# One written order for five engines: prelude, batch 0 and the start of batch 1 of a fused attention and expert kernel

## The chip, the cores and the metric

The kernel runs on one core of one Trainium2 chip. The metric is device time in microseconds (us) of one execution. Five engines run their own instruction lists and wait for each other on semaphores: TensorE (PE in the rows, its weight loads PEld), VectorE (DVE), ScalarE (ACT), GpSimd (POOL) and SyncE (SP), which here issues all transfers.

## What is computed

Three layers follow each other. The first is Nystrom attention over 8 batches, 8 heads, 576 tokens and 64 dimensions, with 32 landmarks (means of 18 tokens) and six steps of a Newton iteration for an inverse:

```python
A, Bm, C = sm(q, k_lm), sm(q_lm, k_lm), sm(q_lm, k)     # softmaxes
Z = Bm.T / (norm_1(Bm) * norm_inf(Bm) + 1e-6)
for _ in range(6):
    Z = 2 * Z - Z @ Bm @ Z
attn = A @ Z @ C @ v
x = silu(attn @ w_gate) * (attn @ w_val) @ w_out        # 512 -> 1536 -> 512
```

The third is a soft mixture of 8 experts with 4 slots each: logits `x @ phi`, a softmax over tokens that gathers 32 slot inputs, two products per expert, and a softmax over slots that spreads the results over the 4608 tokens.

## The kernel before, in words

The output of the attention is never formed. Per batch the kernel makes `WB = Z C v` in small (its last product is `m_w`, its copy L538), multiplies it with a chunk of gate and value weights (`g_product`, L758: `g`), splits `g` in a high part `GH` (ScalarE, L775) and a low part `GL` (VectorE, L789), and multiplies both with the high and low part of the softmax `A` (`EH`, `EL`) in `mm3` (L955). A batch has 12 units, one for each 128 of the 1536 hidden columns. A unit has two halves of 288 tokens; a half is a product `pg` (gate), `u = silu(pg)` on ScalarE (L313), a product `pv` (value) and `hT = u * pv` on VectorE (L984). `hT` goes into the logits (L804) and is transposed into `HB` (L809). There are two buffers each of `pg`, `pv`, `u` and `hT`.

The **prelude** (`first_attention`) does batch 0's attention with nothing of the units beside it: landmark sums of q and k (L334), score products `m_a` and `m_c` (L544) and the 32x32 landmark scores (L378), their softmax (`nrm`, L310, L448 to L451), block-diagonal tiles `bd` (L323), the norms `nx` and the factor `rc` (L477, L328), the first Newton tile (L482), five squarings `m_n` whose halves are copied by VectorE (L505) and ScalarE (L506), products `m_T`, then `VD` (L529) and `m_w`. The softmax of A runs beside it, with subtractions, multiplications and the low part `EL` on GpSimd (L730, L733, L736).

In the prelude and batch 0 the weights are prepared too. They lie in memory as 64-bit numbers. Gate and value weights come in 12 chunks of 1 MB (`HB` or `wr`, L204), the output weights in 12 of 512 KB (L215). A conversion has a ScalarE pass (L177), for some chunks another one (L184), and VectorE passes (L193 with L194, or L190). The output weights are then transposed (`m_wt`), multiplied with phi (`m_p`, `m_ps`) and stored back. The 12 chunks of both kinds must be ready unit by unit in batch 0, where the attention of batch 1 runs as well.

What sets the order: the code is traced in one sequence, with the side work placed by the numbers in `SCHED`. A scheduler then orders each engine's instructions, held by `keep_order` for TensorE from the first unit on (L1154) and for ScalarE within batch 0 (L1115), and by single constraints `issue_after`. The order is fixed when the program is built; on the chip each engine takes its list in order.

Of the kernel before, what the change touches and what calls it, by code (L numbers as in the profile page):

```python
# [51 lines left out]
}  # L52


@with_exitstack
def nystrom_softmoe_kernel(
    ctx: ExitStack,
# [13 lines left out]
    nc = tc.nc  # L71
    pe, act, dve, pool, sp = nc.tensor, nc.scalar, nc.vector, nc.gpsimd, nc.sync

    def keep_order(engine, start, end):

        last = None
        for i in nc.cur_bb.bb.instructions[start:end]:
            if i.engine == engine:
                if last is not None:
                    tc.add_manual_dep(i, last.name, mybir.DependencyInfo(  # L80
                        mybir.DependencyClass.NoSync, mybir.DependencyReason.DATA), reason="keep_order")
                last = i

    def open_pool(name, bufs=1, **kw):
        return ctx.enter_context(tc.tile_pool(name=name, bufs=bufs, **kw))
# [71 lines left out]
    def load_four(nm, b):  # L157

        for hp in range(4):
            t = ap.tile([128, S], F32, tag="qk", name=f"{nm}{b}_{hp}", bufs=4)  # L160
            sp.dma_start(t, (qT if nm == "q" else kT)[b, hp])
            qk_t[nm, b, hp] = t

    def load_v(b):
        t = ap.tile([128, 5, DM], F32, tag="v", name=f"v{b}", bufs=1)
        sp.dma_start(t[:, 0:4, :], v[b, 0:512].rearrange("(c p) d -> p c d", p=128))
        sp.dma_start(t[0:64, 4, :], v[b, 512:576])
        v_t[b] = t
# [32 lines left out]
    def load_w(j):  # L201
        g = W_STAGE[j]
        t = (big(g, f"wr{j}") if g[0] == "w" else part(int(g[0]), int(g[1]))).bitcast(U64)
        sp.dma_start(t, w_cat[j])  # L204
        raw["w", j] = t
# [86 lines left out]
    for j in range(NJ):  # L292
        for kind in "wo":
            first, span = S_[kind][j]
# [8 lines left out]


    fence = {}

    def in_order(kind, *a, **kw):
        other = fence.get("exp" if kind == "silu" else "silu")
        if other is None:
            i = act.activation(*a, **kw)  # L310
        else:
            with tc.issue_after(other):
                i = act.activation(*a, **kw)  # L313
        fence[kind] = getattr(i, "ins", i)

# [14 lines left out]

    def landmark(nm, b, hp, dst):

        with tc.issue_after(fence["hT" if b == 2 else "sum"]) if "sum" in fence else nullcontext():
            dve.tensor_reduce(dst[:, hp, :], qk_t[nm, b, hp].rearrange("p (m s) -> p m s", s=SEG),  # L334
                              axis=AX.X, op=ALU.add)

# [9 lines left out]
    def e_tiles(b):  # L346
        r = []
        for low in range(2):
            p, tag = e_space(b, low)
            r.append(p.tile([128, 2 * S], F32R, tag=tag, name=tag).rearrange("p (q s) -> p q s", q=2))  # L350
        E_t[b] = r
# [356 lines left out]
    def a_softmax(b, qs=(0, 1)):  # L708
        AN, mxA = A_t[b]

        assert b == 0 or ("A", b, 1) in seq
        bc = {q: mxA[:, q, :].unsqueeze(2).to_broadcast([128, SEG, M]) for q in qs}
        at = {}

        def inv(q):
            mx = mxA[:, q, :]
            with tc.issue_after(fence["stat" if b > 1 else "hT"]) if b else nullcontext():
                dve.tensor_reduce(mx, AN[q], axis=AX.X, op=ALU.add)
            dve.tensor_scalar(mx, mx, 1e-9, None, ALU.add)
            dve.reciprocal(mx, mx)  # L720

        def back(q):
            at[q] = ap.tile([128, S], F32, tag="AT", name="AT", bufs=2)
            if b not in E_t:
                e_tiles(b)
            with tc.issue_after(fence["hT"]) if b == 1 else nullcontext():
                dve.transpose(at[q].rearrange("p (t r) -> p t r", r=32), AN[q])

        for f in (lambda q: dve.tensor_reduce(mxA[:, q, :], AN[q], axis=AX.X, op=ALU.max),
                  lambda q: pool.tensor_tensor(out=AN[q], in0=AN[q], in1=bc[q], op=ALU.subtract),  # L730
                  lambda q: in_order("exp", AN[q], AN[q], AF.Exp, scale=SC / SEG),
                  inv,
                  lambda q: pool.tensor_tensor(out=AN[q], in0=AN[q], in1=bc[q], op=ALU.mult),  # L733
                  back,
                  lambda q: act.copy(E_t[b][0][:, q, :], at[q]),
                  lambda q: pool.tensor_tensor(out=E_t[b][1][:, q, :], in0=at[q], in1=E_t[b][0][:, q, :],  # L736
                                               op=ALU.subtract)):
            for q in qs:
                f(q)
                yield  # L740
        if 1 in qs:
            seq.add(("asm", b))
# [35 lines left out]
    def g_unit(b, j):  # L778

        if not paired(b, j):  # L780
            g_product(b, j, 1)
        elif j % 2 == 0:
            g_product(b, j, 2)
# [3 lines left out]
    def g_low():  # L787
        for GL, g, GH in gl_todo:
            dve.tensor_tensor(out=GL, in0=g, in1=GH, op=ALU.subtract)  # L789
        gl_todo.clear()  # L790
# [4 lines left out]
    def logits(b, j, hT):  # L795
        if j == 0:
            L_t[b] = psp.tile([128, 512], F32, tag="l", name="l")
        assert j in p_done
        L = L_t[b]
        seq.add(("l", b, j))  # L800
        main = hT.rearrange("p (k c r) -> p k c r", k=5, c=4)
        for c in range(4):
            k = 5 if c < 2 else 4
            pe.matmul(L[32 * c:32 * c + 32, 0:32 * k], P_sb[:, j, :], main[:, 0:k, c, :],  # L804
                      start=j == 0, stop=j == NJ - 1)

    def transposes(b, j, hT):
        seq.add(("h", b, j))
        dve.transpose(HB[b % 2][:, S * j:S * j + S].rearrange("p (t r) -> p t r", r=32),  # L809
                      hT[:, 0:S].rearrange("p (t r) -> p t r", r=32))  # L810
# [192 lines left out]
    for x in S_["loads"]:  # L1003
        k, n = x[0], x[1:]
# [21 lines left out]
                next(gens[c], None)  # L1026

    m = psp.tile([128, 512], F32, tag="l", name="warm")
    for _ in range(14):
        pe.matmul(m[0:1, 0:1], one, one, start=True, stop=True)  # L1030
    first_attention(side)
    in_order("silu", warm, one, AF.Silu)
# [27 lines left out]
    last = nb - 1  # L1060
# [20 lines left out]
    def tail_loads(b, n):  # L1081
        if b == last - 1 and n == 47:
            attn_stack.close()
            fwp.append(open_pool("fw", side="right", reuse_waits="tile"))
            for t in range(NW):
                ffn_prefetch(t)
        if b == last:
            if n == 26:
                for t in range(NW, NW + 3):
                    ffn_prefetch(t)  # L1090
            if n % 8 == 6:
                i = n // 8
                if i < 3:
                    wo_load(i)
                elif i < 6:
                    ffn_prefetch(NW + i)
# [12 lines left out]
            todo[48 * a + r].append(sm)  # L1109
    prev = None  # L1110
    n_ins = lambda: len(nc.cur_bb.bb.instructions)
    middle = n_ins()
    for b in range(nb):
        if b == 1:
            keep_order(mybir.EngineType.Activation, middle, n_ins())  # L1115
        for j in range(NJ):
            p = prev
            def slot(i):
                n = 4 * j + i
                sg, sl, st_, first = S_["u0" if b == 0 else "u"]  # L1120
                if first:
                    for gen in todo[48 * b + n]:
                        next(gen, None)
                if i == sg and j + 1 < NJ:
                    g_unit(b, j + 1)
                if i == sl and p:
                    logits(*p)
                if i == sg + 1:
                    g_low()
                if i == st_ and p:  # L1130
                    transposes(*p)
                if b == 0:
                    for f in side_w[n]:
                        f()
                if (b, n) == (0, 1):
                    load_w(5)
                if b == 0 and nb > 2:
                    if n == S_["lq"]:
                        assert ("q", 1) in seq
                        load_four("k", 2)  # L1140
                    if n == S_["lv"]:
                        assert ("v", 1) in seq
                        load_v(2)
                tail_loads(b, n)
                if not first:
                    for gen in todo[48 * b + n]:
                        next(gen, None)
                if n == 45 and b + 1 < nb:
                    g_unit(b + 1, 0)
                if n == 46:  # L1150
                    g_low()

            prev = (b, j, *unit(b, j, slot))
    keep_order(mybir.EngineType.PE, middle, n_ins())  # L1154
    in_order("exp", warm, one, AF.Exp)
    logits(*prev)
    transposes(*prev)
# [205 lines left out]
```

## Time and profile before

| | us |
|---|---|
| median of 3 runs (lowest, highest) | 658.64 (657.75, 659.1) |
| the profiled execution, its own time | 659.78 |
| its span, first to last instruction | 658.0 |
| TensorE busy, VectorE busy, ScalarE busy, GpSimd busy in it | 622.5, 468.6, 302.2, 72.3 |

The profiled execution is 1.14 us above the median; 1.78 us of it lie outside the span. A busy engine in this table is one for which the profile shows an instruction under way, and a matmul's shown end is modelled, so short waits of TensorE can lie inside its busy time.

### The profile page before, as it was taken

What the parts mean: (1) busy time and instruction counts of PE and PEld (TensorE: products, weight loads), DVE (VectorE), ACT (ScalarE), POOL (GpSimd) and SP (SyncE); (2) the same over time, 40 slices, a digit from 0 to 9 for tenths busy, and PEclk for the clock granted to TensorE, in tenths of its full rate; (3) what the DMA queues carried; (4) which work ended last, traced back from release to release, by engine and by line L of the source; (5) the groups of instructions that cost most, each with busy time, mean ns of one, the idle gap of its engine ahead of it and who ended that gap; (6) DMA issues with size and microseconds to landing.
All of it is one profiled execution on the core that took longest, in us unless ns stands there. A gap on an engine that the chain in (4) does not pass through costs nothing. (4 is left out here: it accounts for less than half of the span.)

```text
span 658.0 us, 18310 instructions
## 1 busy us (share of the span) xinstructions
PE 622.5 (95%) x7587; PEld 471.1 (72%) x7587; DVE 468.6 (71%) x1139; ACT 302.2 (46%) x761; POOL 72.3 (11%) x81
## 2 busy tenths in 40 slices
PE   7899999999999999999999999999999999999990
PEld 4765678777777787778787778777878877743660
DVE  5898989987678597859785978697866656550441
ACT  2657976365338233823482347234723442311540
POOL 0401012003013001300130013001300000010100
PEclk9799989999999999999999999999999999999996
DMA  8998872542031223112321241122220696599998
GB/s 308 387 327 278 291 248 86 160 148 86 1 99 63 74 75 122 51 63 73 115 73 48 74 143 24 68 73 74 58 89 2 196 376 225 189 333 347 348 371 306
DMA packets 63299, 106.48 MB, mean 162 GB/s; under 512 B 4976, under 2 KB 33008, under 8 KB 61680
## 3 DMA queue, kind: packets, MB, share of 16 engines
q1 hardware_dynamic: 63216, 105.32, 47.7%
q8 instruction: 59, 0.97, 0.6%
q14 instruction: 24, 0.20, 0.1%
HBM read 91.24 MB, written 12.58 MB: 158 GB/s over the span
## 5 line engine op out<-in xcount | busy, mean ns | idle before, releaser
L313 ACT ACTIVATE u<-pg 128x288 f32<-128x288 f32 x169 | 69.7, 412 | 156.4 <-PE pg L955 152.7
L984 DVE TENSOR_TENSOR hT<-u,pv 128x288 f32<-128x288 f32 x169 | 75.8, 448 | 42.3 <-PE pv L955 36.7
L955 PE MATMUL pg<-EH,GH 128*128 128x288 f32 x384 | 94.2, 326 | 0.5 <-ACT GH L775 0.5
L789 DVE TENSOR_TENSOR GL<-g,GH 128x512 fp32r<-128x512 f32 (+1 forms) x114 | 64.7, 597 | 37.0 <-ACT GH L775 36.9
L955 PE MATMUL pg<-EH,GL 128*128 128x288 f32 x384 | 85.3, 299 | 1.7 <-DVE GL L789 1.2
L955 PE MATMUL pv<-EL,GH 128*128 128x288 f32 x384 | 82.4, 296 | 0.0
L955 PE MATMUL pv<-EH,GH 128*128 128x288 f32 x384 | 82.4, 296 | 0.0
L955 PE MATMUL pg<-EL,GH 128*128 128x288 f32 x384 | 82.3, 296 | 0.0
L955 PE MATMUL pv<-EH,GL 128*128 128x288 f32 x384 | 82.1, 295 | 0.0
L775 ACT CAST GH<-g 128x512 fp32r<-128x512 f32 (+1 forms) x114 | 53.4, 520 | 55.3 <-PE g L758 55.2
L955 PEld LDWEIGHTS pg<-EH,GH 128*128 128x128 f32 x384 | 59.6, 190 | 24.7 <-issue 20.3
L809 DVE STREAM_TRANSPOSE HB<-hT 128x576 f32<-128x576 f32 x96 | 74.3, 774 | 1.8
L955 PEld LDWEIGHTS pg<-EH,GL 128*128 128x128 f32 x384 | 62.4, 188 | 4.3 <-DVE GL L789 4.2
L955 PEld LDWEIGHTS pv<-EH,GH 128*128 128x128 f32 x384 | 61.8, 189 | 0.0
L955 PEld LDWEIGHTS pv<-EH,GL 128*128 128x128 f32 x384 | 61.8, 189 | 0.0
L955 PEld LDWEIGHTS pg<-EL,GH 128*128 128x128 f32 x384 | 61.8, 189 | 0.0
L955 PEld LDWEIGHTS pv<-EL,GH 128*128 128x128 f32 x384 | 61.7, 189 | 0.0
L758 PE MATMUL g<-w,WB 64*32 64x512 f32 (+1 forms) x912 | 56.7, 534 | 0.5 <-DVE w L190 0.5
L804 PEld LDWEIGHTS l<-hT,P_sb 128*32 128x32 f32 x768 | 15.2, 108 | 43.8 <-DVE hT L984 14.9
L804 PE MATMUL l<-hT,P_sb 128*32 128x160 f32 (+1 forms) x768 | 44.8, 298 | 1.4 <-DVE hT L984 1.1
L923 PE MATMUL m_d<-HB,HB 32*32 32x384 f32 x864 | 35.3, 491 | 0.0
L923 PE MATMUL m_d<-HB,DN 32*32 32x384 f32 x288 | 35.1, 491 | 0.0
(254 smaller groups left out, 955.8 us busy)
## 6 DMA issues: line engine op xcount, KB each, us to landing
k<-in_kT_dram SPq DMA_DIRECT2D x52, 288.0 KB, 3.7
ffn<-in_w_dram SPq DMA_DIRECT2D x13, 1024.0 KB, 8.3
ffn<-in_w_dram SPq DMA_DIRECT2D x24, 512.0 KB, 9.0
HB<-in_w_cat_dram SPq DMA_DIRECT2D x8, 1024.0 KB, 7.7
v<-in_v_dram SPq DMA_DIRECT2D x8, 1024.0 KB, 6.0
q<-in_qT_dram SPq DMA_DIRECT2D x28, 288.0 KB, 3.0
HB<-in_w_out_dram SPq DMA_DIRECT2D x12, 512.0 KB, 5.3
wr<-in_w_cat_dram SPq DMA_DIRECT2D x4, 1024.0 KB, 8.8
```

Source lines behind the costliest of these rows:

```text
L313: i = act.activation(*a, **kw)
L758: pe.matmul(gs[r][32 * hp:32 * hp + 32, 0:256 * n].rearrange("p (u f) -> p u f", u=n), WB[b % 2][64 * r:64 * r + 64, hp, :], w[64 * r:64 * ...
L775: act.copy(H_, g)
L789: dve.tensor_tensor(out=GL, in0=g, in1=GH, op=ALU.subtract)
L804: pe.matmul(L[32 * c:32 * c + 32, 0:32 * k], P_sb[:, j, :], main[:, 0:k, c, :], start=j == 0, stop=j == NJ - 1)
L809: dve.transpose(HB[b % 2][:, S * j:S * j + S].rearrange("p (t r) -> p t r", r=32), hT[:, 0:S].rearrange("p (t r) -> p t r", r=32))
L923: pe.matmul(ms[a][32 * g:32 * g + 32, 0:384].rearrange("p (j f) -> p j f", j=NJ), d_of(a, g, k), hb[32 * a:32 * a + 32, :, 4 * k + g, :], ...
L955: pe.matmul(ps[:, 0:HALF], G_t[b, j, q, sel_][h], e[:, q, ts_], start=n == 0, stop=n == 5)
L984: i = dve.tensor_tensor(out=o, in0=u, in1=pv[:, 0:HALF], op=ALU.mult)
```

## The change

`ORDER` holds a list of numbers for each engine. A number is an instruction's place among those traced for that engine, and `a+n` is a run of n from place a. `written_order` chains the listed instructions in that order. The lists have 928 entries for TensorE, 263 for VectorE, 182 for ScalarE, 18 for GpSimd and 72 for SyncE, and cover the prelude, batch 0 and the first units of batch 1. What is not listed comes behind the last listed one, on TensorE in traced order, on the others as the scheduler puts it. The two calls of `keep_order` go. The `issue_after` constraints of activation functions, landmarks and A's softmax are dropped for what is traced before unit 1 of batch 1. Two one-column warm-up products are added (14 to 16). No other instruction is added or removed, and no tile changes its buffer.

```diff
+ORDER = {
+    'DVE': '''
+      1 0 4 3 2 6 5 7 24 12 61 9 8 10 23 14+2 11 17 22 16 18+3 27 21 13 42+2 25+2 32+7 41 29 39 44+2 49 46
...
+    def written_order():
+        for name, runs in ORDER.items():
+            traced = [i for i in nc.cur_bb.bb.instructions if i.engine == getattr(mybir.EngineType, name)
+                      and type(i).__name__.startswith("Inst")]
+            first, last = [], None
+            for r in runs.split():
+                a, n = (int(x) for x in (r + "+1").split("+")[:2])
+                first += traced[a:a + n]
+            for i, before in zip(first[1:], first):
+                behind(i, before)
+            seen = {i.name for i in first}
+            last = first[-1]
+            for i in traced:
+                if i.name not in seen:
+                    behind(i, last)
+                    if name == "PE":
+                        last = i
...
-    for _ in range(14):
+    for _ in range(16):
         pe.matmul(m[0:1, 0:1], one, one, start=True, stop=True)
...
-    middle = n_ins()
     for b in range(nb):
-        if b == 1:
-            keep_order(mybir.EngineType.Activation, middle, n_ins())
         for j in range(NJ):
+            if (b, j) == (1, 1):
+                written[0] = False
...
-    keep_order(mybir.EngineType.PE, middle, n_ins())
+    written_order()
```

Lines of the changed kernel stand about 60 higher than those of before (L505 becomes L567, L194 becomes L252, L184 becomes L242).

**VectorE, from the norms to the first Newton tile, and the five squarings.** Before, from the maximum over C's scores on (`CE`; `mxA` and `AN` belong to A's softmax):

```order
L395 TENSOR_REDUCE stat<-CE_159 128x1
L477 TENSOR_REDUCE nx<-m_nx 128x4
L396 TENSOR_SCALAR stat<-stat 128x1
L718 TENSOR_REDUCE mxA<-AN_156 128x18
L328 TENSOR_SCALAR rc<-nx 128x1 x2
L719 TENSOR_SCALAR mxA<-mxA 128x18
L395 TENSOR_REDUCE stat<-CE_160 128x1
L329 RECIPROCAL rc<-rc 128x2
L720 RECIPROCAL mxA<-mxA 128x18
L482 SCALAR_TENSOR_TENSOR newton<-m_n,rc,cst 128x128 x2
```

In the change, the same stretch:

```order
L791 TENSOR_REDUCE mxA<-AN_158 128x18
L457 TENSOR_REDUCE stat<-CE_162 128x1
L458 TENSOR_SCALAR stat<-stat 128x1
L457 TENSOR_REDUCE stat<-CE_161 128x1
L458 TENSOR_SCALAR stat<-stat 128x1
L539 TENSOR_REDUCE nx<-m_nx 128x4
L390 TENSOR_SCALAR rc<-nx 128x1 x2
L391 RECIPROCAL rc<-rc 128x2
L544 SCALAR_TENSOR_TENSOR newton<-m_n,rc,cst 128x128 x2
```

Nothing stands between the norms and the Newton tile any more. The second reduction of `mxA`, for which GpSimd's subtractions wait, has moved from ahead of the scaling of `nrm` to behind it.

**VectorE, from the last squaring's copy to the first unit's low parts, in the change** (L567 is the copy, L251 and L252 are conversion passes of weight chunk `w_251`, L396 landmark sums of batch 1):

```order
L567 COPY newton<-m_n 128x128
L251 TENSOR_SCALAR w_251<-w_251 128x512 x2
L252 SCALAR_TENSOR_TENSOR w_251<-HB_84,w_251 128x512
L396 TENSOR_REDUCE qs<-q_1_113 128x32
L396 TENSOR_REDUCE ks<-k_0_111 128x32
L591 TENSOR_SCALAR VD<-m_v_445,rc 128x64 x2
L252 SCALAR_TENSOR_TENSOR w_251<-HB_84,w_251 128x512
L396 TENSOR_REDUCE ks<-qk_123 128x32
L252 SCALAR_TENSOR_TENSOR w_251<-HB_84,w_251 128x512
L851 TENSOR_TENSOR GL<-g,GH 128x256 x2
```

Before, `VD` follows the last copy directly and the conversion of that chunk is done ahead of both; now five 512-column passes of it and two landmark sums stand between and behind.

**ScalarE, around the first squaring's copy.** Before:

```order
L177 ACTIVATE HB_85<-HB_85 128x512
L310 ACTIVATE CE_160,stat<-CE_160,stat 128x576
L506 COPY newton<-m_n 128x128
L313 ACT_TABLE_LOAD
L313 ACTIVATE warm<-one 1x1
L177 ACTIVATE w_249<-HB_84 128x1024
L495 COPY newton<-m_T 128x256
```

In the change (`wr_131` is the raw chunk 4 of the gate and value weights, not touched here before):

```order
L372 ACTIVATE CE_161,stat<-CE_161,stat 128x576
L372 ACTIVATE AN_159<-AN_159 128x576
L242 ACTIVATE wr_131<-wr_131 128x1024
L568 COPY newton<-m_n 128x128
L472 COPY CT<-m_t 128x512
L235 ACTIVATE w_668<-wr_131 128x1024
L568 COPY newton<-m_n 128x128
```

The load of the activation table for silu has gone from here to just ahead of the first unit's `u`, and a pass over chunk 4 stands ahead of the copy.

## Rows read from the trace of the kernel before

**Rows 1.** Windows of four stages: us; PE, PEld, DVE, ACT, POOL; clock, DMA share, GB/s.

```profile
0.00:39.49 39.49, 31.43 (x325) 22.77 (x325) 29.58 (x69) 17.94 (x43) 9.02 (x14) 0.91 0.96 348
39.49:122.58 83.09, 78.67 (x869) 60.96 (x869) 74.68 (x167) 60.96 (x137) 8.76 (x7) 0.98 0.68 233
122.58:190.88 68.30, 66.50 (x859) 51.70 (x858) 53.44 (x132) 31.02 (x81) 10.58 (x10) 1.00 0.30 92
190.88:256.04 65.16, 64.98 (x827) 51.08 (x825) 51.19 (x127) 29.35 (x77) 8.27 (x8) 1.00 0.25 78
```

**Rows 2.** Timeline of TensorE: the first product of batch 0 and of batch 1.

```profile
39.49 0.68 PE L955 MATMUL pg<-EH,GH 128*128 128x288 f32 x2 [0.52 <-ACT GH L775]
...
122.58 0.52 PE L955 MATMUL pg<-EH,GH 128*128 128x288 f32 x2
```

**Rows 3.** Waits of VectorE up to 123 us: us in total, times, longest.

```profile
DVE qs L334 <- DMA q<-in_qT_dram: 3.9, 2, 3.6
DVE GL L789 <- ACT GH L775: 3.3, 3, 1.4
DVE AN L390 <- PE m_a L544: 2.3, 1, 2.3
DVE newton L505 <- PE m_n L471: 2.1, 2, 1.1
DVE u L970 <- ACT u L969: 1.2, 1, 1.2
DVE hT L984 <- ACT u L313: 1.1, 2, 0.7
...
DVE VD L529 <- PE m_v L526: 0.6, 1, 0.6
...
DVE AN L390 <- ACT nrm L310: 0.4, 1, 0.4
```

**Rows 4.** Timeline of VectorE in the prelude: start, us, instructions.

```profile
14.59 0.12 DVE L448 TENSOR_SCALAR stat<-stat 128x2 f32<-128x2 f32 x1
...
16.37 1.82 DVE L451 TENSOR_SCALAR nrm<-nrm,stat 128x32 f32<-128x32 f32 x2
...
18.64 0.38 DVE L455 TENSOR_SCALAR nrm<-cst,stat 128x32 f32<-128x32 f32 x2
...
31.33 1.16 DVE L194 SCALAR_TENSOR_TENSOR w<-HB,w 128x512 int32<-128x512 int32 x1
32.41 1.37 DVE L519 TENSOR_SCALAR stat<-stat 128x2 f32<-128x2 f32 x1
...
35.60 0.48 DVE L529 TENSOR_SCALAR VD<-m_v,rc 128x64 f32<-128x64 f32 x2 [0.56 <-PE m_v L526]
```

**Rows 5.** Timeline of GpSimd in the prelude: the subtractions and the low parts.

```profile
15.88 2.27 POOL L730 TENSOR_TENSOR AN<-AN,mxA 128x576 f32<-128x576 f32 x2 [14.71 <-DVE stat L449]
...
30.52 3.23 POOL L736 TENSOR_TENSOR EL<-AT,EH 128x576 fp32r<-128x576 f32 x2 [4.82 <-ACT EH L735]
```

**Rows 6.** Groups of ScalarE's instructions up to 122.58 us: busy us, mean ns.

```profile
L313 ACT ACT_TABLE_LOAD x3 | 3.8, 1283 | 0.1
...
L184 ACT ACTIVATE wr<-wr 128x1024 int32<-128x1024 uint16 x2 | 2.3, 1164 | 0.0
```

**Rows 7.** Windows, columns as in rows 1: the first 20 us, and a stretch at the lower clock.

```profile
0.00:10.00 10.00, 6.39 (x71) 2.88 (x74) 5.53 (x8) 1.49 (x2) 0.58 (x7) 1.00 0.84 295
10.00:20.00 10.00, 8.99 (x84) 6.59 (x74) 7.28 (x23) 4.45 (x11) 2.27 (x2) 1.00 0.95 349
22.60:29.40 6.80, 5.91 (x27) 5.31 (x27) 4.73 (x13) 5.14 (x11) 2.42 (x3) 0.50 1.04 381
```

**Rows 8.** Transfers issued up to 125 us: KB each, median us to landing.

```profile
HB<-in_w_cat_dram SPq DMA_DIRECT2D x8, 1024.0 KB, 7.7
HB<-in_w_out_dram SPq DMA_DIRECT2D x12, 512.0 KB, 5.3
wr<-in_w_cat_dram SPq DMA_DIRECT2D x4, 1024.0 KB, 8.8
...
q<-in_qT_dram SPq DMA_DIRECT2D x8, 288.0 KB, 3.3
...
cst<-in_consts_dram SPq DMA_DIRECT2D x1, 209.0 KB, 5.7
```

More of the change, by code (lines that the diff above doesn't have):

```diff
@@ L52 @@
 }
+ORDER = {
+    'PE': '''
[7 rows of a table added]
+      788+4 820+6 832+8 814+6 826+6 844+12 862+6 872+16 856+6 888+8 840+4 896+6 920+8''',
+    'DVE': '''
[8 rows of a table added]
+      239 242+2 238 241 240 247+2 255 252 256+2 253 259 249 246 258 262 261''',
+    'Activation': '''
[5 rows of a table added]
+      162 167 166 168+2 171 173 170 174 172 175 181 177 176 180 179''',
+    'Pool': '''
+      0 2+6 1 8 10 9 11 16 12 15 13+2 17''',
+    'SP': '''
+      0+2 5 2+2 7 4 6 14 26 8 15 18 10 25 22 17 16 20 9 23 11+3 40 24 19 21 29+2 28 32+2 31 34 36 35 37+3
+      42 41 58 43 45 44 27 46 59+2 47+2 61 50+2 49 64 52 65 53 56+2 66+2 54 68+3 55 62 71''',
+}
 @with_exitstack
@@ L82, in keep_order, with behind @@
                 last = i
+    def behind(i, before):
+        tc.add_manual_dep(i, before.name, mybir.DependencyInfo(
+            mybir.DependencyClass.NoSync, mybir.DependencyReason.DATA), reason="order")
+    def written_order():
[15 more added lines that the diff above has]
+                        last = i
     def open_pool(name, bufs=1, **kw):
@@ L305, in nystrom_softmoe_kernel, with behind_it @@
     fence = {}
+    written = [True]
+    def behind_it(i):
+        return nullcontext() if i is None or written[0] else tc.issue_after(i)
     def in_order(kind, *a, **kw):
@@ L311, in in_order @@
         else:
-            with tc.issue_after(other):
+            with behind_it(other):
                 i = act.activation(*a, **kw)
@@ L331, in landmark @@
     def landmark(nm, b, hp, dst):
-        with tc.issue_after(fence["hT" if b == 2 else "sum"]) if "sum" in fence else nullcontext():
+        with behind_it(fence.get("hT" if b == 2 else "sum")):
             dve.tensor_reduce(dst[:, hp, :], qk_t[nm, b, hp].rearrange("p (m s) -> p m s", s=SEG),
@@ L716, in inv @@
             mx = mxA[:, q, :]
-            with tc.issue_after(fence["stat" if b > 1 else "hT"]) if b else nullcontext():
+            with behind_it(fence.get("stat" if b > 1 else "hT")):
                 dve.tensor_reduce(mx, AN[q], axis=AX.X, op=ALU.add)
@@ L725, in back @@
                 e_tiles(b)
-            with tc.issue_after(fence["hT"]) if b == 1 else nullcontext():
+            with behind_it(fence["hT"] if b == 1 else None):
                 dve.transpose(at[q].rearrange("p (t r) -> p t r", r=32), AN[q])
```

19 rows, old and new, of the table ORDER are left out of this document.

## The prediction

> **What bounds the kernel now.** I read the stages first. The windows [rows 1] cut the span where the first `pg` product of batch 0 and of batch 1 starts [rows 2]: a prelude of 39.49 us, batch 0 with 83.09, batch 1 with 68.30, and batch 2 with 65.16, in which TensorE is busy 64.98. Every later full batch is TensorE's; nothing of the change reaches it. What is to be won lies ahead of 190.88 us. There the engine to watch is VectorE. In batch 0 it is busy 74.68 of 83.09 us against 51.19 in batch 2, since the weight conversions come on top. In the prelude it is busy 29.58 of 39.49. TensorE's 78.67 of 83.09 in batch 0 says less: shown matmul ends are modelled, so the busy time can hold waits.
>
> VectorE's idle time ahead of batch 1 is 39.49 - 29.58 + 83.09 - 74.68 = 18.32 us. The work that VectorE has to do before batch 1 can start is nearly the same list in both orders, so the time to batch 1 changes by what this idle time, and stretched instructions, change. The view of its waits [rows 3] says where they lie: 3.9 us at the start for q's first transfers, which no order removes; 2.3 for the first scores; 2.1 for squarings in the Newton iteration; 3.3 for `GH`, the cast of `g`; 1.2 and 1.1 for ScalarE's `u`; 0.6 and 0.4 for `VD` and `nrm`. The timeline [rows 4] shows stretched ones: L451 took 1.82 us for two instructions where L455, the same form, took 0.38, and L519 took 1.37 where L448, the same form, took 0.12. Each ended with a GpSimd product [rows 5]: L451 at 18.19 with the subtractions' 18.15, L519 at 33.78 with `EL`'s 33.75.
>
> **The change part by part.** *Gains.* (1) The landmark scores now come ahead of C's scores on TensorE, and one conversion pass and two transposes stand on VectorE between the scores and their softmax. Of the 2.3 us for the scores I take 1.3 (the scores of the last landmark still have to be made) and all 0.4 for `nrm`: 1.7. Bounds 0.4 and 2.7. (2) Between two copies of the Newton tile there are now other instructions of VectorE throughout, and two landmark sums ahead of `VD`: the 2.1 and 0.6 us become work, 2.7. They are hidden by conversions that batch 0 needs anyway. If those conversions' data came late, that cover would be gone and 0 would be left. (3) `mxA`'s second reduction moved behind the scaling of `nrm`, and GpSimd's subtractions wait for it, so L451 cannot meet them: 1.82 - 0.38 = 1.4 us. L519 (1.25 us too long) now stands ahead of the transposes that feed `EL`; I count half, 0.6, as other GpSimd work can meet it. Together 2.0; bounds 0 and 2.65. (4) `GH`: in the new list landmark sums and conversion passes stand ahead of `GL` at the first units; I take half of 3.3, 1.6. Bounds 0 and 3.3. (5) `u`: the two halves of a gate product are now made ahead of the value products in the first unit, which gives ScalarE more time; of 1.2 + 1.1 I take 1.0. Bounds 0 and 2.3. The sum of gains is 1.7 + 2.7 + 2.0 + 1.6 + 1.0 = 9.0 us.
>
> *Costs.* (6) The pass over chunk 4 (`wr`) stands ahead of ScalarE's copy of the first squaring: 1.16 us of L184 [rows 6] on the chain of squarings, 1.2 in full; nothing, if VectorE's list is the longer one there. Queued behind it are the copies of all later squarings, for which TensorE waits. (7) Two passes L252 of the chunk that the first `g` needs now stand behind `VD`, where landmark sums stood. `EL`, two products of 1.6 us [rows 5], runs at about that time. L194, the same operation, stood beside `EL` at 31.33 and took 1.16 us, ending 1.26 us before `EL` did [rows 4, 5], so it need not wait for both products. I take one product, 1.6, with 0 and 3.2 as bounds. (8) The table load of silu, 1.28 us [rows 6], goes from the prelude to the place ahead of the first `u`. ScalarE has by then two weight passes, two casts and a copy listed behind the casts for the first product, and TensorE has both `pg` and both `pv` products, so I take nothing; without that cover 1.3. (9) The two extra warm-up products lie ahead of the first landmark, under the wait for q: nothing. (10) Output weights now load ahead of the constants. The constants, 209 KB, then come after 8 x 288 and 512 KB, with phi 3.2 MB; with 2.95 MB moved in the first 10 us [rows 7, 8] they are there at about 10.6 us and first needed for the warm-up products behind the scores: nothing. The costs are 2.8 us.
>
> (11) The granted clock: 6.8 us of the squarings ran at 0.5, that is 1.2 GHz [rows 7]; in the new order the squarings are as thin for TensorE. I take no difference. Matmuls are short against the waits there, so the bound either way is a quarter of that stretch, 1.7 us. (12) Batch 1 took 3.14 us more than batch 2. From its unit 1 on TensorE's order is the old one and VectorE has 15 us to spare, so I take nothing; bounds -3.1 and +2.
>
> The Trainium skill, page "SBUF — State Buffer", section on what contends, says that VectorE and GpSimd share one pair of ports as an exclusive lock, and that a two-input VectorE instruction fully waits for a GpSimd instruction that reads memory. L519's end with `EL`'s agrees, and the page would make each L252 that meets `EL` wait for the end of the product it meets; taken to the end it is the second rival below.
>
> The sum is 659.78 - 9.0 + 2.8 = 653.6 us for an execution like the profiled one, which lay 1.14 us above the median of the runs shown. So the forecast is 652.4.
>
> **The rivals.** *More is won.* If VectorE never waits but for the first transfers and some 2.5 us more, the gain is 18.32 - 3.9 - 2.5 = 11.9: 646.7. For it speaks that steady batches keep TensorE at 65 us, so the units themselves have room; against it that `u` and `GH` waits are hand-overs between engines that a written order can only fill if there is work ready.
>
> *GpSimd takes the gain.* More conversion passes now lie in the prelude, and GpSimd is busy 9.02 us there. If both products of `EL` are waited for (1.6 more) and the credit for L451 and L519 comes back as other stretched passes (2.0), the gain is 6.2 - 3.6 = 2.6: 656.0. Against it: GpSimd's subtractions, the other long pair [rows 5], cannot meet L451 any more, and before too conversions ran beside `EL`.
>
> *Nothing changes.* TensorE's busy 78.67 of 83.09 us in batch 0 could be real work; then the 4.42 us left are all that batch 0 holds, and an earlier prelude is given back as conversions and their loads catch up: 658.6. Against it: batch 2 has the same 12 units plus a softmax stage that batch 0 lacks, in 65.16 us.
>
> *Slower.* The pass over chunk 4 on ScalarE waits for its transfer, and every later copy of the Newton tile is queued behind it. Its load is fifteenth in SyncE's list, behind 8 x 288, 512, 209, 1024, 512 and 288 KB; with its own 1024 that is 6.0 MB, which at 295 and 349 GB/s [rows 7, 8] has landed at 18.7 us. The first squaring is ready at about 19. Each us later moves the whole iteration; at 26 us the forecast's gain of 6.2 is gone and from 27 on the kernel is slower by more than 0.2%. For it: a `wr` transfer took 8.8 us from issue to landing [rows 8], and SyncE must first wait for the landmark scores to free q's buffer. With 3 us beyond break-even, 661.6.
>
> **How the numbers follow.** The forecast 0.46 (its own range 649 to 655.5), more won 0.12, GpSimd takes it 0.20, nothing changes 0.09, slower 0.13. Faster by over 0.2% are the first three, 0.78; 0.2% (1.3 us) is about what a measurement of this kernel can tell from none. The range leaves out the best of the second case and the worst of the last: 645 to 659.5.
>
> **What would show it.** After the change the first `pg` should start at about 35 us instead of 39.49, and batch 1's at 116 to 117 instead of 122.58, with batch 1 itself still near 68 and batch 2 at 65.2. VectorE's waits for the Newton tile and `VD` should be under 0.5 us each, the two instructions of L451 (L513 then) under 0.5 us together. Step 7 is right if a pass L252 near `VD` lasts over 1 us and ends with `EL`. The prediction is wrong if the first `pg` moves but batch 1's does not, or if ScalarE's pass over chunk 4 starts after 22 us with a wait for its transfer.

## The result and the profile after

The change runs in 651.92 us (median of 4 runs, 651.27 to 654.04) against 658.27 (657.75 to 659.1) for the kernel before: a ratio of 0.9911, 95% interval 0.9887 to 0.9935. The profiled execution took 652.49 us with a span of 650.5.

The stages first, in the windows between the first `pg` products. Columns are those of [rows 1]; L1017 is L955 of before.

```profile
0.00:38.64 38.64, 28.67 (x344) 20.36 (x344) 30.30 (x72) 20.65 (x46) 9.68 (x13) 1.00 0.98 369
38.64:114.91 76.27, 74.29 (x851) 58.08 (x845) 70.19 (x162) 56.76 (x131) 8.99 (x8) 1.00 0.66 234
114.91:183.96 69.05, 67.23 (x867) 51.80 (x867) 54.37 (x134) 31.19 (x83) 10.61 (x10) 1.00 0.33 105
183.96:249.11 65.15, 64.98 (x826) 51.08 (x825) 51.18 (x127) 29.35 (x77) 8.29 (x8) 1.00 0.25 78
```

Against [rows 1] the prelude is 0.85 us shorter, batch 0 is 6.82 shorter, batch 1 is 0.75 longer, batch 2 is the same. So batch 1 starts 7.67 us earlier. VectorE's idle time up to there is 38.64 - 30.30 + 76.27 - 70.19 = 14.42 us, 3.90 less than before, and its busy time is 100.49, 3.77 less. The granted clock is shown as 1.00 in all four stages; the stretches at 1.2 GHz, 22.6 to 29.4 us [rows 7] and 84.0 to 87.4 us in the kernel before, are gone. For the first 13.0 us of the change the 1.00 is no reading, though: its first clock record begins there (in the kernel before at 8.95 us), and the last section shows slower products ahead of it.

VectorE's waits up to 115 us (us in total, times, longest; names of lines as in [rows 3], some 62 higher):

```profile
DVE qs L396 <- DMA q<-in_qT_dram: 3.6, 1, 3.6
DVE GL L851 <- ACT GH L837: 2.1, 1, 2.1
DVE AN L452 <- PE m_a L606: 1.5, 1, 1.5
DVE ks L396 <- DMA qk<-in_kT_dram: 0.9, 1, 0.9
DVE u L1032 <- ACT u L1031: 0.9, 1, 0.9
DVE AT L789 <- POOL AN L795: 0.8, 1, 0.8
DVE HB L251 <- ACT HB L235: 0.6, 1, 0.6
DVE bd L385 <- PE m_n L743: 0.6, 2, 0.4
DVE AN L452 <- ACT nrm L372: 0.5, 1, 0.5
DVE nx L730 <- ACT RV L728: 0.4, 1, 0.4
DVE nx L539 <- PE m_nx L521: 0.4, 1, 0.4
DVE stat L715 <- ACT RV L693: 0.3, 1, 0.3
DVE RV L759 <- ACT RV L758: 0.3, 1, 0.3
DVE hT L1046 <- ACT u L375: 0.2, 1, 0.2
DVE newton L567 <- PE m_n L533: 0.2, 1, 0.2
```

The waits for squarings fell from 2.1 to 0.2 us and the one for `VD` is gone. But eight lines of this list (`ks`, `AT`, `HB`, `bd`, both `nx`, `stat`, `RV`) wait for something new or for longer.

VectorE's timeline in the prelude of the change, with the instructions that the prediction spoke of:

```profile
15.11 0.20 DVE L513 TENSOR_SCALAR nrm<-nrm,stat 128x32 f32<-128x32 f32 x1
...
15.55 0.23 DVE L513 TENSOR_SCALAR nrm<-nrm,stat 128x32 f32<-128x32 f32 x1
...
26.00 1.11 DVE L581 TENSOR_SCALAR stat<-stat 128x2 f32<-128x2 f32 x1
...
33.82 0.46 DVE L591 TENSOR_SCALAR VD<-m_v,rc 128x64 f32<-128x64 f32 x2
34.21 1.64 DVE L252 SCALAR_TENSOR_TENSOR w<-HB,w 128x512 int32<-128x512 int32 x1
...
36.43 1.23 DVE L252 SCALAR_TENSOR_TENSOR w<-HB,w 128x512 int32<-128x512 int32 x1
```

And GpSimd's, the three products beside them:

```profile
25.56 3.17 POOL L795 TENSOR_TENSOR AN<-AN,mxA 128x576 f32<-128x576 f32 x2 [3.12 <-ACT CT L475]
33.89 1.40 POOL L798 TENSOR_TENSOR EL<-AT,EH 128x576 fp32r<-128x576 f32 x1 [5.16 <-ACT EH L797]
...
35.42 1.69 POOL L798 TENSOR_TENSOR EL<-AT,EH 128x576 fp32r<-128x576 f32 x1
```

L513 is no longer stretched (1.82 us in [rows 4]). L581, the old L519, still is, now beside the multiplication of `AN`. The two L252 are stretched beside the two products of `EL`.

### The profile page after: what moved, and what is told of

Its sections match the earlier page's. It is cut to its first block, busy times and chain, and to the rows that moved or that the text cites. A ratio compares the mean times of both kernels' runs of the same rounds, so it can differ in the third digit from the quotient of the medians.

```text
span 650.5 us, 18267 instructions
## 1 busy us (share of the span) xinstructions
PE 616.0 (95%) x7591; PEld 465.9 (72%) x7591; DVE 465.8 (72%) x1139; ACT 300.8 (46%) x761; POOL 73.2 (11%) x81
## 5 line engine op out<-in xcount | busy, mean ns | idle before, releaser
L1017 PE MATMUL pg<-EH,GH 128*128 128x288 f32 x384 | 92.9, 323 | 0.0
L1017 PE MATMUL pg<-EH,GL 128*128 128x288 f32 x384 | 84.5, 297 | 0.5
L1017 PE MATMUL pv<-EH,GH 128*128 128x288 f32 x384 | 84.0, 300 | 0.0
L1017 PE MATMUL pg<-EL,GH 128*128 128x288 f32 x384 | 82.1, 295 | 0.0
L1017 PE MATMUL pv<-EL,GH 128*128 128x288 f32 x384 | 82.0, 295 | 0.0
L1017 PE MATMUL pv<-EH,GL 128*128 128x288 f32 x384 | 81.9, 294 | 0.0
L1017 PEld LDWEIGHTS pg<-EH,GH 128*128 128x128 f32 x384 | 59.4, 189 | 23.6 <-issue 20.4
L1017 PEld LDWEIGHTS pg<-EH,GL 128*128 128x128 f32 x384 | 62.0, 188 | 2.6 <-DVE GL L851 2.6
L1017 PEld LDWEIGHTS pv<-EH,GH 128*128 128x128 f32 x384 | 61.2, 188 | 3.7 <-issue 2.5
L1017 PEld LDWEIGHTS pv<-EH,GL 128*128 128x128 f32 x384 | 61.5, 188 | 0.0
L1017 PEld LDWEIGHTS pg<-EL,GH 128*128 128x128 f32 x384 | 61.5, 188 | 0.0
L1017 PEld LDWEIGHTS pv<-EL,GH 128*128 128x128 f32 x384 | 61.5, 188 | 0.0
```

The costliest lines, as they stand in the source:

```text
L1017: pe.matmul(ps[:, 0:HALF], G_t[b, j, q, sel_][h], e[:, q, ts_], start=n == 0, stop=n == 5)
```

## The experiments

The runs differ in order, in unused products and in one transfer's place. Times of one kernel lie 1 to 5 us apart, partly by stages that no edit touches, so the starts of the stages say more; but each comes from one profiled execution, and differences of a few tenths of a us show nothing. Starts of batch 0, 1 and 2, in us, with the median of all executions and the ratio to the kernel before on the same chip:

| run | batch 0 | batch 1 | batch 2 | median (lowest to highest) | ratio, 95% interval |
|---|---|---|---|---|---|
| before | 39.49 | 122.58 | 190.88 | | |
| the change | 38.64 | 114.91 | 183.96 | 651.92 (651.27 to 654.04) | 0.9911 (0.9887 to 0.9935) |
| e1_cold | 40.16 | 118.19 | 187.66 | 654.02 (651.91 to 656.72) | 0.9947 (0.9925 to 0.9969) |
| e2_before_fill | 41.91 | 122.99 | 190.53 | 659.44 (658.08 to 660.49) | 1.0033 (1.0016 to 1.0050) |
| e3_no_dve | 45.55 | 126.52 | 195.81 | 664.45 (662.97 to 665.83) | 1.0115 (1.0077 to 1.0153) |
| e4_no_sp | 55.86 | 132.67 | 200.98 | 670.17 (669.16 to 671.74) | 1.0205 (1.0172 to 1.0237) |
| e5_swap | 37.94 | 113.94 | 182.78 | 652.00 (651.54 to 653.64) | 0.9901 (0.9886 to 0.9916) |
| e6_act242 | 38.95 | 115.02 | 184.46 | 652.73 (652.02 to 653.51) | 0.9906 (0.9891 to 0.9921) |
| e7_silu | 39.78 | 115.73 | 184.88 | 653.59 (652.93 to 654.54) | 0.9921 (0.9908 to 0.9934) |
| e8_cut | 38.66 | 115.22 | 183.31 | 651.05 (650.72 to 652.11) | 0.9883 (0.9869 to 0.9897) |
| e9_swap_cut | 37.47 | 115.20 | 183.73 | 651.68 (649.69 to 652.10) | 0.9898 (0.9875 to 0.9921) |
| e10_early | 37.40 | 115.13 | 184.44 | 654.16 (653.16 to 655.21) | 0.9941 (0.9921 to 0.9961) |
| e11_all | 37.31 | 114.42 | 182.04 | 652.13 (651.15 to 653.33) | 0.9911 (0.9890 to 0.9931) |
| e12_load_first | 37.21 | 113.58 | 181.73 | 650.71 (650.04 to 652.79) | 0.9901 (0.9874 to 0.9927) |

**Is it VectorE or TensorE's clock?** My theory was the prediction's: VectorE's waits and stretches. The rival was that the gain is the vanished stretches at 1.2 GHz. `e1_cold` takes TensorE's 16 wide fill products out of the change, four groups of four, and puts one-column products there. `e2_before_fill` adds fill products to the order of before.

```diff
 # e1_cold, in first_attention, four times
-    keep_warm(4)
+    for _ in range(4):
+        pe.matmul(m[0:1, 0:1], one, one, start=True, stop=True)
 # e2_before_fill, before, in the Newton loop
+    for _ in range(6):
+        pe.matmul(mw[:, 0:160], ident, cst[:, 128:288], start=True, stop=True)
     R = NBUF[:, k]
```

> The changed kernel with its 16 warm-up products of 160 columns in the prelude made one column wide (same places, outputs unused in both). Theory 'VectorE': the change wins because VectorE waits less and is stretched less; the clock of TensorE matters little. Then the granted clock may fall to 0.5 for some of the prelude and the time stays within 2 us of the change, 651.5 to 654. Rival 'clock': the change wins because the records show no stretch at 0.5 within its prelude and batch 0, against 6.8 and 3.4 us before. Then a low clock here takes most of the 6.4 us back: 656 to 659.

> The kernel before with six more unused products of 160 columns behind each squaring of the Newton iteration, so that TensorE is not sparse there. Rival 'clock': the stretch at 0.5 in the prelude goes, the first unit starts 2 us or more before 39.5 us, and the time falls to 655 to 656. Theory 'VectorE': the first unit moves by less than 1 us either way and the time stays between 657.3 and 659.5.

`e1_cold` has 10.2 us at 1.2 GHz from 16.3 us on and 3.4 more from 40.2 on, and still starts batch 1 at 118.19, 4.4 us ahead of before. So most of the gain stays without the clock, and the clock is worth 2 to 3 us of it here. `e2_before_fill` ends where the theory put it, but neither side foresaw its prelude, which was to move by less than 1 us or to shrink by 2. It has no stretch at 1.2 GHz up to batch 1, but its prelude is 2.42 us longer and its batch 0 2.01 shorter (81.08 against 83.09), and it ends no earlier. The fill products cost time themselves, so its total doesn't price the clock. Its batch 0 shows something of it: from the seventh unit's first product to the eighth's, where the kernel before has its stretch from 84.0 us, before takes 8.32 us (84.06 to 92.38) and this run 6.83 (85.97 to 92.80).

The kernel before settles the rest, since its clock differs from execution to execution. On the four chips of these experiments it ran 50 times. In 35 of them the mean granted clock is 0.987 or less, and they take 657.28 to 660.12 us, median 658.7; in 12 it is 0.990 or more, and they take 654.65 to 657.20, median 656.0 (three lie between). The change has 0.990 to 0.992 in its four executions, `e1_cold` 0.979 to 0.987 in its ten. Four medians thus stand side by side:

| | low clock | high clock |
|---|---|---|
| order of before | 658.7 | 656.0 |
| written order | 654.0 (`e1_cold`) | 651.9 |

The order is worth 4.1 to 4.7 us at either clock, and the clock 2.1 to 2.7 us in either order. `e2_before_fill`, at 0.987 to 0.992, lies 3.4 us above the 656.0: that is the price of its fill products. The groups were made after the runs, by the clock that each execution happened to have; that an edit which takes the clock away, `e1_cold`, costs about as much speaks for the clock as the cause.

VectorE's rows say which part is which. Windows of `e1_cold` for its prelude and batch 0, and two of VectorE's waits up to 118.2 us:

```profile
0.00:40.16 40.16, 27.53 (x344) 19.46 (x344) 30.50 (x72) 20.67 (x46) 9.68 (x13) 0.87 0.97 357
40.16:118.19 78.03, 76.31 (x851) 59.23 (x845) 69.65 (x162) 56.85 (x131) 8.99 (x8) 0.98 0.65 229
```

```profile
DVE newton L569 <- PE m_n L535: 1.6, 3, 0.9
...
DVE hT L1048 <- ACT u L375: 0.8, 2, 0.5
```

VectorE's idle time up to batch 1 is 40.16 - 30.50 + 78.03 - 69.65 = 18.04 us in `e1_cold`, 14.42 in the change and 18.32 before. Its busy time is 100.15, 100.49 and 104.26. So with the low clock nearly all of the idle time that the change saved is back, with VectorE's list unchanged; the wait for squarings is 1.6 us again. What stays is the shorter busy time. `e1_cold` has 3.4 us more at 1.2 GHz than the kernel before, so it may overstate the clock's part.

**Which lists carry the gain?** One engine's list is removed, and the scheduler orders that engine.

```diff
 # e3_no_dve
-    'DVE': ''' 1 0 4 3 2 6 5 7 24 12 61 9 8 10 23 14+2 ...''',
 # e4_no_sp
-    'SP': ''' 0+2 5 2+2 7 4 6 14 26 8 15 18 10 25 22 ...''',
```

> The changed kernel without VectorE's list: the scheduler orders VectorE, the other four keep their lists. Theory 'VectorE': most of the gain goes or turns into a loss, 656 to 665, with VectorE's waits ahead of batch 1 back at 18 us or more. Rival 'TensorE and ScalarE': what wins is the order of products and ScalarE passes (both gate products ahead of the value products, A's scores ahead of C's); then the time stays between 651 and 654.

> The changed kernel without SyncE's list: the scheduler orders the transfers, the other four keep their lists. Theory 'VectorE': loads are mostly ahead of need, at most 1.5 us is lost, 651.5 to 653.5. Rival 'loads': the order of the loads is what lets conversions run in the prelude; 655 or more, with ScalarE's conversion passes waiting for transfers.

Both are slower than the kernel before. Without VectorE's list 12.5 us are lost, 6.9 of them in the prelude and 4.7 in batch 0. That isn't VectorE's share of the gain, since the other lists were made for its order. The clock is in both runs too: up to batch 1 they have 10.2 (`e3_no_dve`) and 17.1 us (`e4_no_sp`) at 1.2 GHz. I had expected SyncE's list to be worth little, and that was a miss: without it the prelude is 17.2 us longer. ScalarE's waits in `e4_no_sp` up to 133 us (lines 3 lower than in the change):

```profile
ACT HB L232 <- DMA HB<-in_w_out_dram: 23.2, 4, 16.1
ACT wr L239 <- DMA wr<-in_w_cat_dram: 7.2, 1, 7.2
```

its timeline at the pass over chunk 4:

```profile
38.45 1.10 ACT L239 ACTIVATE wr<-wr 128x1024 int32<-128x1024 uint16 x1 [7.21 <-DMA wr<-in_w_cat_dram]
```

and VectorE's wait for the squaring that follows it:

```profile
DVE newton L564 <- PE m_n L530: 8.9, 4, 6.7
```

The pass over chunk 4 starts at 38.45 us instead of 21.61, ScalarE's Newton copies stand behind it, and VectorE waits 6.7 us for the next squaring. That is the mechanism of my "Slower" rival; SyncE's list, which moves the chunk's load up, prevents it. But it is only part of the 17.2 us. ScalarE's first pass over output weights, which waited 16.1 us for its load, starts at 18.10 instead of 11.22, and the second at 27.92 instead of 17.51. So 10.4 of the 16.8 us by which the pass over chunk 4 is late were lost ahead of it, to loads that the rival doesn't name.

**Three single places of the prediction.** `e5_swap` lets two passes L252 go ahead of `EL` instead of beside it (step 7), `e6_act242` puts the pass over chunk 4 behind the copies of the first two squarings (step 6), `e7_silu` loads silu's table early again (step 8).

```diff
 # e5_swap, VectorE
-  48 28 54 98 65 59+2 30 70 55 63+2
+  48 28 54 30 55 59+2 98 65 70 63+2
 # e6_act242, ScalarE (57 is the pass over chunk 4)
-  38 12 9 8 10 59 11 13 57 17 16 21
+  38 12 9 8 10 11 13 17 59 57 16 21
 # e7_silu, ScalarE (32 is the warm-up of silu, with its table load)
-  38 12 9 8 10 59 11 13 57 17 16 21
+  38 12 9 8 10 32 59 11 13 57 17 16 21
```

> The changed kernel with two passes L252 of the first unit's weight chunk moved from behind VD to ahead of it, and two landmark sums from ahead to behind. In the change these passes took 1.64 and 1.23 us, each to the end of one of GpSimd's two EL products, where 0.68 is usual. If waiting for GpSimd on VectorE's path is what the prediction's step 7 says (1.6 us), the passes take 0.7 us, the first unit starts about 1 us before 38.64 and batch 1 about 1 us before 114.91: 650.5 to 651.3. Rival: the first unit waits for the chain over WB and g anyway, or the lead is lost in batch 0: within 0.5 us of the change.

> The changed kernel with the ScalarE pass over chunk 4 (1.15 us) moved from ahead of the copy of the first squaring to behind the copy of the second. If step 6 is right (1.2 us on the chain of squarings), VD comes about 1 us earlier and so does the first unit: 650.5 to 651.3. Rival 'VectorE': VectorE's list is full between the copies, so the chain has slack; the first unit moves by less than 0.4 us and the time stays within 0.5 us.

> The changed kernel with the warm-up activation of silu, and with it the table load of 1.28 us, put back into the Newton iteration (behind the last exponential of the prelude) instead of just ahead of the first u. Step 8 says that the load is hidden at the first u: no change there or a loss of up to 1.2 us where it now delays the copies of the squarings, 651.5 to 653. Rival: the load is on the path to the first hT; then u starts 1.3 us earlier and 0.5 to 1.3 us are won.

VectorE's timeline in `e5_swap`, at the place of the two stretched passes:

```profile
32.43 1.89 DVE L252 SCALAR_TENSOR_TENSOR w<-HB,w 128x512 int32<-128x512 int32 x3
34.24 0.47 DVE L591 TENSOR_SCALAR VD<-m_v,rc 128x64 f32<-128x64 f32 x2
```

Three passes take 1.89 us, 0.63 each; in the change the two beside `EL` took 1.64 + 1.23, so 1.6 us too much. Step 7 is confirmed in place and in the size of the stretch. Batch 0 starts 0.70 us earlier and batch 1 0.97; the median doesn't show it. `e6_act242` starts batch 0 0.31 us later, not 1.2 earlier. ScalarE's copy of the first squaring starts at 22.62 us there and at 22.63 in the change, while the norms come 0.31 us later than in the change; so the pass held that copy up by some 0.3 us. `e6_act242` moves the pass, it doesn't remove it. `e7_silu` starts batch 0 1.14 later and batch 1 0.82 later; from the first `pg` to batch 1 it takes 75.95 us against 76.27, so where the change has it the load costs at most some 0.3 us.

**What follows, first batch 1.** `e8_cut` ends the written order where the tracing of batch 1 begins, so that batch 1's side work is the scheduler's; `e9_swap_cut` is `e5_swap` and `e8_cut` together.

```diff
 # e8_cut
+        if b == 1:
+            early = {i.name for i in nc.cur_bb.bb.instructions}
-            if (b, j) == (1, 1):
+            if (b, j) == (1, 0):
                 written[0] = False
...
-                first += traced[a:a + n]
+                first += [i for i in traced[a:a + n] if i.name in early]
```

> The changed kernel with all five lists cut where batch 1 is traced: what belongs to batch 1's units comes behind the lists in the old manner. Theory: the part of the lists in batch 1 is worth nothing or costs the 0.7 us by which batch 1 got longer (69.05 against 68.30): 651 to 653. Rival: the lists' part in batch 1 carries batch 0's last units; then 1 us or more is lost, 653 to 656.

> The changed kernel with both the two passes L252 ahead of VD and the lists cut where batch 1 is traced. The two edits act in different stages (prelude and batch 1), so both leads should add: batch 1 starts about 1 us before 114.91 and lasts 68.1, 649.5 to 651. Rival: the lead of the prelude is lost at the border of the lists; then 651 to 652, as with one of them.

Batch 1 takes 68.09 us in `e8_cut` and 68.53 in `e9_swap_cut` instead of 69.05. In `e8_cut` it starts 0.31 us later and batch 2 0.65 earlier, so most of its extra 0.75 comes from the part of the lists that lies in it. But the leads don't add: `e9_swap_cut` is 1.17 us ahead of the change at batch 0 and 0.29 behind it at batch 1. `e10_early` runs nine more unused products ahead of the first scores, and `e11_all` is the three edits together.

```diff
 # e10_early
+    dve.memset(wz, 0.0)
     for _ in range(16):
         pe.matmul(m[0:1, 0:1], one, one, start=True, stop=True)
+    for _ in range(9):
+        pe.matmul(m[:, 0:160], wz[:, 0:128], wz, start=True, stop=True)
```

> The changed kernel with nine unused products of 160 columns on a zeroed tile in TensorE's idle time ahead of the landmark scores (six before the first score product, three behind the first two). In the change the granted clock is shown at full only from 13.02 us (before: from 8.95), and score products of 288 columns took 0.69 us until then, 0.43 after. If that late clock is why the prelude won only 0.85 us, the scores are ready about 1 us earlier and the first unit starts 0.7 to 1.2 us before 38.64. Rival: the clock stays low until 13 us or the lead is lost to transfers that conversions wait for; the first unit moves by less than 0.4 us.

> The changed kernel with all three: the two passes ahead of VD, the lists cut where batch 1 is traced, and nine unused products ahead of the landmark scores. If all three leads add, 648.5 to 650.5; if the early products do nothing, as with the other two alone.

The prelude of `e10_early` is 1.24 us shorter, and its batch 0 is 1.47 longer. So leads of about 1.2 us at batch 0's start were lost inside it twice. The first products of the units say where: against the change, `e9_swap_cut` is 1.18 us ahead at the fourth unit (55.09 against 56.27), 0.56 at the fifth (63.46 against 64.02) and 0.18 at the sixth (70.20 against 70.38). The last 0.5 us goes at the cut: from the twelfth unit to batch 1 both runs with the cut take 2.9 us, the change 2.43.

The first loss, in the fourth unit, is a late transfer. ScalarE's pass over a chunk that was issued at 48.27 us waits for it, and VectorE for the pass; in the change that pass, at 56.21 us, waits for no transfer:

```profile
56.03 1.13 ACT L235 ACTIVATE w<-HB 128x1024 f32<-128x1024 f32 x1 [0.89 <-DMA HB<-in_w_cat_dram]
```

```profile
57.19 0.43 DVE L251 TENSOR_SCALAR w<-w 128x512 int32<-128x512 int32 x1 [1.05 <-ACT w L235]
```

For the second, in the fifth unit, SyncE's timeline of `e9_swap_cut` shows

```profile
53.93 5.14 SPq L273 DMA_DIRECT2D HB<-in_w_out_dram  x2
59.12 0.42 SPq L306 DMA_DIRECT2D wo_dram<-HB  x1
59.64 0.38 SPq L219 DMA_DIRECT2D k<-in_kT_dram  x1
60.07 0.48 SPq L262 DMA_DIRECT2D wr<-in_w_cat_dram  x1
```

and ScalarE's

```profile
67.92 1.15 ACT L235 ACTIVATE w<-wr 128x1024 f32<-128x1024 f32 x1 [1.95 <-DMA wr<-in_w_cat_dram]
```

The load of chunk 9 goes out at 60.07 and ScalarE's pass over it waits 1.95 us, to 67.92. In the change the pass waits 1.56, to 68.08; in `e10_early` 2.60, to 68.35. So it starts within 0.4 us in all three, whatever the lead (in `e5_swap` and `e11_all` at 67.1, after waits of 1.29 and 1.93; these two still are 0.95 and 0.98 us ahead of the change at the sixth unit). The buffer was free at 55.1, when VectorE's L248 had ended, but the second output-weight load ahead of it in SyncE's list waited for VectorE. `e12_load_first` is `e9_swap_cut` with chunk 9's load ahead of that one:

```diff
-  ... 35 37+3 42 41 58 43 45 44 27 46
+  ... 35 37+3 43 42 41 58 45 44 27 46
```

> This is the run with both the swap and the cut, and one more transfer moved: in SyncE's list the load of weight chunk 9 into wr goes ahead of the second of two output-weight loads. In that run the chunk was issued at 60.07 us, since an output-weight load ahead of it waited for VectorE until 58.7, though its own buffer was free at 55.1; ScalarE's pass over it then waited 1.95 us and started at 67.92, and the lead of 1.17 us that the prelude had handed on was still 1.18 us at the fourth unit (55.99 against 57.17) and 0.18 at the sixth (70.20 against 70.38). Theory that this late load takes the lead: the load is issued by 56.5, the pass starts by 66.3 without a wait for it, the sixth unit starts by 69.5 and batch 1 at 113.8 to 114.5 instead of 115.20; time 650 to 651.3. Rival, that batch 0 is paced by something else there (VectorE's own list, or another chunk): the pass starts earlier but batch 1 still starts at 114.9 to 115.4, time 651 to 652.5. A third outcome: the output-weight load that is now second is late itself, and a wait for it comes in place of the other.

SyncE's timeline in `e12_load_first`:

```profile
55.10 0.33 SPq L262 DMA_DIRECT2D wr<-in_w_cat_dram  x1
57.71 0.33 SPq L273 DMA_DIRECT2D HB<-in_w_out_dram  x1
```

ScalarE's, at the pass over chunk 9 and the one ahead of it:

```profile
64.24 0.69 ACT L235 ACTIVATE HB<-HB 128x512 f32<-128x512 f32 x1 [1.61 <-DMA wo_dram<-HB]
65.58 1.18 ACT L235 ACTIVATE w<-wr 128x1024 f32<-128x1024 f32 x1
```

The pass starts at 65.58 without a wait for its transfer, the sixth unit at 68.56 and batch 1 at 113.58, 1.62 us ahead of `e9_swap_cut`. The theory held for the part that lies at this transfer, queued behind a load that waited for something else: from the fifth unit to the sixth this run takes 5.77 us, `e9_swap_cut` 6.74. The other 0.67 us are there at the fifth unit already (62.79 against 63.46), ahead of the pass: the transfer that was late in the fourth unit isn't late here, and the edit doesn't touch it. For `e10_early`, which shows the same wait for chunk 9, the edit wasn't tried. Part of the third outcome came too: the pass ahead of it now waits 1.61 us for a store. This run has the earliest starts of batch 1 and batch 2 and the lowest median of all; its ratio overlaps with the change's.

## Why the prediction was right, and where its steps were off

**What bounds the kernel** was right in place: the whole gain lies ahead of batch 1, in VectorE's idle time and stretched instructions, and batch 2 on is as before. The forecast of 652.4 meets 651.92, but in part by luck: the clock, put at nothing, gave 2 to 3 us, while the gains that I counted came out smaller (table).

| step | taken | measured | by |
|---|---|---|---|
| (1) scores, `nrm` | 1.7 | 0.7 | waits 2.3 + 0.4 to 1.5 + 0.5 |
| (2) squarings, `VD` | 2.7 | 2.5; 1.1 without the clock | waits 2.1 + 0.6 to 0.2 + 0; to 1.6 + 0 in `e1_cold` |
| (3) L451, L519 | 2.0 | 1.7 | 1.82 to 0.20 + 0.23; 1.37 to 1.11 |
| (4) `GH` | 1.6 | 1.2 | wait 3.3 to 2.1 |
| (5) `u` | 1.0 | 1.2; 0.2 without the clock | waits 1.2 + 1.1 to 0.9 + 0.2; to 1.3 + 0.8 in `e1_cold` |
| (6) pass over chunk 4 | -1.2 | 0 to -0.3 | `e6_act242` |
| (7) L252 beside `EL` | -1.6 | -1.6; -1.0 at batch 1 | `e5_swap` |
| (8) silu's table | 0 | 0 to -0.3 | `e7_silu` |
| (11) clock | 0 | 2 to 3 | `e1_cold`; before at either clock |
| (12) batch 1 | 0 | -0.75 | windows; `e8_cut` |

**Steps 2 and 5** reached their size, but not by their mechanism alone. I let other work of VectorE cover the waits for squarings and more time for ScalarE cover those for `u`. In `e1_cold`, with that same order, most of these waits are back. The order by itself removed the wait for `VD` and 0.7 us more; at its low clock the five gains come to 4.9 us instead of 9.0.

**Step 3** went wrong in one half: L519 kept 1.11 us, as I had allowed for, since it met the other long GpSimd pair (25.56 to 28.73). L451 went as said.

**Step 6** failed: the pass is at most 0.3 us of the chain. VectorE is busy between the squarings in either order and waits for them 0.2 us in both runs, so a later ScalarE copy hides behind it, which was the bound of zero that I named and didn't take.

**Step 7** was right. The two L252 end at 35.85 and 37.66 us, near the ends of the two products of `EL`, 35.29 and 37.11. The Trainium skill, page "SBUF — State Buffer", section "Who interferes with whom", has a VectorE instruction with two SBUF inputs fully wait for a GpSimd instruction that reads SBUF and started first. Here the trace agrees: each L252 started after its `EL` product had, and they ended 0.56 and 0.55 us after it, close to the 0.63 that a pass takes by itself. Both products were met, not one, for the price of one. L519, which the prediction took as a sign of that rule, has one input, so it isn't an instance of it.

**Step 8** is seen in ScalarE's timeline of the change:

```profile
21.61 1.15 ACT L242 ACTIVATE wr<-wr 128x1024 int32<-128x1024 uint16 x1
...
40.65 1.28 ACT L375 ACT_TABLE_LOAD   x1
41.95 0.41 ACT L375 ACTIVATE u<-pg 128x288 f32<-128x288 f32 x1
```

The load is followed by `u` at once and TensorE has `pg` and `pv` products to go on with. The first row answers the "Slower" rival: the pass over chunk 4 starts at 21.61 us without a wait. Its load also had more room than I gave it: VectorE's copy of the first squaring starts at 22.21 us in the change (23.00 before), not at about 19.

**Step 11** was mis-sized, and it is the largest miss: I let the order be as thin for TensorE as before and saw no low stretch go; both went. My bound of 1.7 us counted only the stretch in the prelude, not the one at 84.0 us; measured are 2.1 to 2.7 us. Why none occurs in the change I can't tell from these runs beyond `e1_cold`, where they come back without the fill products. The kernel before has the same fill products and keeps the high clock only in some executions.

**What had no term** evened out. VectorE's waits for `pv` in the trace before,

```profile
DVE hT L984 <- PE pv L955: 1.0, 2, 0.8
...
DVE hT L982 <- PE pv L955: 0.4, 1, 0.4
```

went to zero, and those for q fell by 0.3. Against it come 3.4 us of new or longer waits in the list of the change: `AT` for GpSimd 0.8, `HB` for ScalarE 0.6, `ks` 0.4 more, and five lines with 0.2 to 0.4 more. Waits thus fell by 0.7 + 2.5 + 1.2 + 1.2 + 1.4 + 0.3 - 3.4 = 3.9 us, the change in idle time, of which `e1_cold` keeps 0.3. Of the 3.77 us less of busy time, some 1.0 are two instructions of batch 0's last unit, an `hT` and a transpose, that now lie behind batch 1's start; the rest are instructions that are less stretched (L451 alone 1.4), less the 1.6 us by which the two L252 are stretched more.

**The split by stage was wrong**: I put the first `pg` at about 35 us and batch 1 at 116 to 117; they came at 38.64 and 114.91. I let the removed waits shorten the prelude. There the waits for q, scores, `nrm`, squarings and `VD` fell by 3.5 us, but 1.6 came new (`AT`, `ks` and `nx`), and VectorE's busy time rose from 29.58 to 30.30 us, with the two stretched L252 and 15 conversion passes instead of 13. `VD` moved from 35.60 to 33.82, the first `pg` by 0.85. Batch 0 won 2.33 us of idle time, where the low stretch at 84.0 us is gone, and 4.49 of busy time, with two conversion passes fewer, those last two instructions gone and less stretch. My test "the first `pg` moves but batch 1's does not" had the sides the wrong way round.

**The rivals.** "More is won" would have needed 11.9 us. "GpSimd takes the gain" has its mechanism (step 7, L581) but not its size. "Nothing changes" falls with batch 0's 6.82 us. "Slower" is what `e4_no_sp` shows when the transfers aren't ordered with the rest.

## What to carry to other kernels

A wait that goes with a new order isn't yet the order's gain: the clock moved too, and only a run of the same order at the low clock told the two apart. Where one kernel has run at two granted clocks, its own executions price the clock. Read idle and busy time stage by stage; a wait removed in one stage can be replaced there and the gain appear in the next. Order the transfers together with the engines that wait for them: late loads at the head of an in-order list cost 17 us in `e4_no_sp`, and one behind a blocked load cost about 1 us in `e9_swap_cut`. When a lead vanishes, compare the starts of the units one by one; an instruction that starts at nearly the same time in every variant, whatever came before it, is where to look.

## What the hardware showed that I had not expected

The score products of 288 columns are slower in the change than in `e10_early`. TensorE's timeline of the change, and then of `e10_early`, at the same products:

```profile
8.99 0.69 PE L606 MATMUL m_a<-qk,ks 64*32 64x288 f32 x2
```

```profile
8.85 0.43 PE L614 MATMUL m_a<-qk,ks 64*32 64x288 f32 x2
```

Nine wide products ahead of them make the difference, 0.69 us against 0.43. The windows give a granted clock of 1.00 for the first 10 us of the change all the same, so this early stretch is read from the products' durations, not from the clock. The first clock record of `e10_early` begins at 5.9 us, that of the change at 13.0. A VectorE instruction on two columns took 1.11 us beside a GpSimd multiplication (L581) where its like took 0.12 [rows 4]: the stretch follows GpSimd's work, not the instruction's size. It doesn't befall every instruction beside that pair: L248, with two inputs, came next, at 27.03 us, and took 0.68, while the pair ran to 28.73.
